# One weight load cut into two contraction halves, and two others joined, in a fused layernorm, state-space and SwiGLU kernel

## The chip, the cores and the metric

The kernel runs on one core of a Trainium2 chip. The metric is the device time of one execution in microseconds (us), taken as the median of several runs. A separate execution was recorded by the hardware profiler; all rows of the profile come from that one execution. Engines are named as the profile names them: PE (matrix products) with PEld (its weight loads), DVE (vector), ACT (activations and copies), POOL, and SP, which here only issues transfers. A "q" behind an engine's name (SPq) marks the issuing of a transfer and not the transfer itself.

## The reference

```python
x = A_x                                  # 1 x 2048 x 512, bf16
xn = _layernorm(x, axis=-1)
return x + _A_ref(xn, ...) + _B_ref(xn, w_gate, w_up, w_down)

def _B_ref(x, w_gate, w_up, w_down):     # 512 -> 1376 -> 512
    g = _silu(x @ w_gate)
    u = x @ w_up
    return (g * u) @ w_down
```

`_A_ref` is a diagonal complex state-space layer: an input projection with `B`, a recurrence over the 2048 positions, an output projection with `C`, and a skip term. Both branches read the same normalised input `xn`.

## The kernel before

The 2048 rows of x are cut into 16 tiles of 128 rows, and four tiles make a chunk of 512, so there are four chunks. The contraction over the 512 model columns is cut into four slices k = 0 to 3 of 128; `HK` is 2, half of them. The 1376 hidden columns make ten blocks `fi` of 128 and a last one of 96. The order on every engine is the order in which the program is written: nothing is moved later by a planner, and each engine works its list from top to bottom, waiting where an operand has not come.

**Loads.** Lines 123 to 142 issue the first loads. All but one go to SP: tile 0 of x (line 123), the gate weights of group 0 (`wg_g[0]`, blocks 0 and 1, line 126), the up weights of group 0 (`wu_g[0]`, line 127), tiles 2 and 3 of x (lines 128 and 129), then gate and up of group 1 (block 2, lines 130 and 131) and of group 2 (blocks 3 to 6, lines 136 and 137), and two transposing loads of `B_re` (line 139). Tile 1 of x goes out on ACT (line 125). The helper `load_w1` loads one group of one weight with one transfer; all its transfers carry line 113 in the profile. Each weight tile is laid out as partition, slice k, column. `load_mid` (line 144) follows later on SP, behind the transposing move of tile 3 (line 259). `load_late` (line 155) issues tiles 8 to 15 of x and then the down weights `wd_sb` in two transfers: blocks 0 to 4 and blocks 5 to 9 (lines 159 and 160). `wd_sb` is read by the output products (lines 566 and 592). Right behind `load_late` SP issues eight transposing loads of `C` (line 877).

**The head on PE.** While the first loads are under way PE runs dummy products (line 670). Tile 0 is normalised on DVE and transposed on PE (`xT_pe`, line 245), and its transpose is copied out by DVE (line 252) and ACT (line 254). Then the products of chunk 0 begin column by column through `head_mm` (line 693), whose arguments are the weight (0 gate, 1 up), the range of tiles, the slices k and the blocks:

```python
head_mm(0, 0, 1, range(0, HK), (0, 1))   # gate, k 0-1
head_mm(1, 0, 1, range(0, HK), (0,))     # up, k 0-1: first use of wu_g[0]
xT_pe(1)
rstd_act(2)
head_mm(0, 0, 1, range(HK, KD), (0, 1))
head_mm(1, 0, 1, range(0, HK), (1,))
head_mm(1, 0, 1, range(HK, KD), (0, 1))  # up, k 2-3
```

Behind them come the same products for tile 1, block 2 for tiles 0 and 1, the transposes of tile 2 (`xT_pe(2, on_dve=(0, 1))`, whose copies both go to DVE), the up products of block 2, and the products of tile 2. From line 763 on the blocks 3 to 6 follow at line 455, gate first, then up.

**The head on DVE.** In order: statistics of tiles 0 and 1, their normalisation (line 222), the statistics of tile 2 (line 205, with tile 2 of x as operand), half of the statistics of tile 3 (line 721), the normalisation of tile 2 (line 222), the other half for tile 3 (lines 723 and 724), and the two copies of the transposed tile 2 (line 252).

Of the kernel before, what the change touches and what calls it, by code (L numbers as in the profile page):

```python
# [23 lines left out]
def kernel(  # L24
# [17 lines left out]
    nc = tc.nc  # L42
# [9 lines left out]
    KD = D // 128  # L52
    HK = KD // 2
    NQ = Pst // 128
    FT = (F + 127) // 128
# [27 lines left out]
    wu_v = B_w_up.rearrange("(k p) f -> p k f", p=128)  # L83
# [5 lines left out]
    fgroups = [(0, 2), (2, 3), (3, 7), (7, FT - 1)]  # L89
    wg_g, wu_g = [], []  # L90
# [6 lines left out]
    wd_sb = const.tile([128, FT - 1, D], BF16, name="wd_sb")  # L97
# [13 lines left out]
    def load_w1(q, tiles, view, gi):  # L111
        a, b = fgroups[gi]
        q.dma_start(out=tiles[gi][:], in_=view[:, :, a * 128:min(F, b * 128)])  # L113
# [10 lines left out]
    nc.vector.memset(xall[:, 1, 0:D // 2], 0.0)  # L124
    nc.scalar.dma_start(out=xall[:, 1, :], in_=x_v[:, 1, :])
    load_w1(nc.sync, wg_g, wg_v, 0)
    load_w1(nc.sync, wu_g, wu_v, 0)
    nc.sync.dma_start(out=xall[:, 2, :], in_=x_v[:, 2, :])
    nc.sync.dma_start(out=xall[:, 3, :], in_=x_v[:, 3, :])
    load_w1(nc.sync, wg_g, wg_v, 1)  # L130
# [24 lines left out]
    def load_late():  # L155
        nc.scalar.dma_start(out=wu_last[:], in_=wu_v[:, :, FL:FL + LB])
        nc.sync.dma_start(out=xall[:, 2 * TPC:NT, :], in_=x_v[:, 2 * TPC:NT, :])
        wd_v = B_w_down[0:FL, :].rearrange("(k p) d -> p k d", p=128)
        for a, b in ((0, FT // 2), (FT // 2, FT - 1)):
            nc.sync.dma_start(out=wd_sb[:, a:b, :], in_=wd_v[:, a:b, :])  # L160


    ones = nc.const_aps.tensor(1.0, (128, CW), BF16)
# [692 lines left out]
    for part in range(2):  # L856
        for q in range(NQ):
# [10 lines left out]
           ["ln2"] * len(norm2) + ["ln3"] * (len(stats3) + len(norm3)))  # L868
    queue("cf", c_ops())
    load_late()  # L870
    for fi in range(G0, FT):
        gateup_tile(0, fi)
# [55 lines left out]
```

## Time and profile before

| | |
|---|---|
| median of 3 runs | 178.29 us (178.04 to 178.75) |
| the profiled execution | 178.63 us, of which the span from the first to the last instruction is 176.8 us |
| instructions | 2598 |
| busy: PE, PEld | 172.1 us, 83.4 us |
| busy: DVE, ACT, POOL | 153.8 us, 96.4 us, 51.8 us |
| granted TensorE clock | 1.000 |
| transfers | 16.36 MB in 31292 packets |

Rows of the timeline give start, duration, engine, line, operation, the tile written and the tile read, the shape and the number of merged instructions; what stands in brackets at the end is the idle time of the engine just before, and what ended it. Rows of transfers give the size and the time from issue to landing, that is, until the last of the data is in place. The chain of waits is followed back from the last instruction, at each step to what released it.

### The profile page before, as it was taken

To read this page: it belongs to the slowest core of one execution; us is meant where nothing else is said; L and a number is where in the kernel's file an instruction comes from. 1 tells how busy PE (TensorE), PEld (TensorE's weight loads), DVE (VectorE), ACT (ScalarE), POOL (GpSimd) and SP (SyncE) were. 2 spreads that over 40 slices of the span, in tenths; PEclk is the share of its full clock that TensorE was granted. 3 is DMA by queue.
4 is the path that set the end of the run, shared out by engine and by line. 5 is a ranking of instruction groups with operands and counts; after the bars stand their busy time and mean duration, and the time that the engine had idled before them with its cause. 6 is when DMAs were issued, how large, how long until landed. Compare 5 with 4: busy or idle time off the path is not lost.

```text
span 176.8 us, 2598 instructions
## 1 busy us (share of the span) xinstructions
PE 172.1 (97%) x939; PEld 83.4 (47%) x954; DVE 153.8 (87%) x235; ACT 96.4 (55%) x178; POOL 51.8 (29%) x86
## 2 busy tenths in 40 slices
PE   8999999999999999999999999999999999999993
PEld 3877544444444444444444444444444444444443
DVE  4779998999999997999999999999999999981033
ACT  5397899867698679714666661053866610001300
POOL 6050120001400220019998040058476510001410
PEclk9999999999999999999999999999999999999999
DMA  5998497995431013900000020029799300000652
GB/s 164 305 186 197 91 247 97 336 272 117 88 73 21 0 30 89 356 4 17 17 19 19 0 85 7 0 23 126 88 126 188 64 6 0 0 4 0 64 99 75
DMA packets 31292, 16.36 MB, mean 92 GB/s; under 512 B 20208, under 2 KB 31088, under 8 KB 31248
## 3 DMA queue, kind: packets, MB, share of 16 engines
q1 hardware_dynamic: 24704, 11.51, 27.5%
q0 software_dynamic: 5184, 4.07, 16.0%
q10 hardware_dynamic: 1392, 0.62, 1.2%
q8 instruction: 7, 0.11, 0.3%
q14 instruction: 5, 0.04, 0.1%
HBM read 8.33 MB, written 5.24 MB: 77 GB/s over the span
## 4 chain that ended last, share of the span: by engine, by line
PE 94%; DMA 2%; issue 1%; SPq 0%; DVE 0%
PE ps L455 35%; PE ps L604 16%; PE ps L380 16%; PE ps L566 10%; PE ps L592 10%; DMA wu<-in_B_w_up_dram 2%; PE ps L693 2%; PE ps L513 2%; PE ps L774 2%; PE ps L555 2%; PE ps L502 1%; PE ps L245 0%; SPq L113 0%; SPq L123 0%; DVE res L609 0%
## 5 line engine op out<-in xcount | busy, mean ns | idle before, releaser
L455 PE MATMUL ps<-xnT,wu 128*128 128x512 bf16 (+1 forms) x144 | 36.3, 373 | 0.2
L455 PE MATMUL ps<-xnT,wg 128*128 128x512 bf16 (+1 forms) x145 | 36.3, 373 | 0.2
L422 DVE TENSOR_TENSOR_SCAN g<-r_t,car,u 128x512 bf16<-128x512 f32 x24 | 28.8, 1263 | 0.0
L380 PE MATMUL ps<-xnT,BT 128*128 128x512 bf16 x126 | 28.2, 379 | 0.1
L604 PE MATMUL ps<-CF,wt 128*128 128x512 bf16 (+2 forms) x140 | 27.6, 355 | 0.4 <-issue 0.3
L474 ACT ACTIVATE guT<-ps 128x512 bf16<-128x512 f32 (+1 forms) x40 | 23.6, 590 | 5.9 <-PE ps L455 5.8
L475 ACT CAST u<-ps 128x512 bf16<-128x512 f32 (+1 forms) x40 | 23.0, 576 | 6.5 <-PE ps L455 6.4
L617 ACT CAST res<-ps 128x512 bf16<-128x512 f32 x12 | 6.7, 590 | 36.1 <-PE ps L604 26.8
L455 PEld LDWEIGHTS <-wu 128*128 128x128 bf16 x148 | 14.5, 98 | 16.6
L188 POOL DMA_DIRECT2D gu_rows<-ul x36 | 17.7, 499 | 15.8 <-DVE ul L490 15.8
L455 PEld LDWEIGHTS <-wg 128*128 128x128 bf16 x148 | 14.4, 98 | 16.5
L382 ACT CAST u<-ps 128x512 bf16<-128x512 f32 x32 | 18.2, 586 | 6.0 <-PE ps L380 5.9
L618 POOL DMA_DIRECT2D out_dram<-res x12 | 10.5, 1221 | 36.2 <-ACT res L617 36.1
L604 PEld LDWEIGHTS <-wt 128*128 128x128 bf16 x144 | 13.3, 98 | 15.0 <-issue 1.3
L380 PEld LDWEIGHTS <-BT 128*128 128x128 bf16 x128 | 12.5, 98 | 14.9 <-issue 0.3
L214 POOL TENSOR_TENSOR rstd<-ve,neg_half 128x2 f32<-128x2 f32 (+1 forms) x4 | 5.7, 1418 | 44.9 <-DVE ve L213 44.9
L592 PE MATMUL ps<-wd_sb,guT 128*128 128x512 bf16 x79 | 17.5, 379 | 0.1
L566 PE MATMUL ps<-wd_sb,guT 128*128 128x512 bf16 x79 | 17.4, 379 | 0.1
L470 DVE TENSOR_TENSOR guT<-guT,u 128x1024 bf16<-128x1024 bf16 x20 | 13.4, 678 | 0.0
L566 PEld LDWEIGHTS <-guT 128*128 128x128 bf16 x80 | 7.8, 98 | 9.5
L592 PEld LDWEIGHTS <-guT 128*128 128x128 bf16 x80 | 7.8, 98 | 9.5
L205 DVE BATCH_NORM_STATS2 stats<-xall 128x6 f32<-128x512 bf16 x14 | 9.5, 678 | 2.7 <-DMA xall<-in_A_x_dram 2.7
(125 smaller groups left out, 201.4 us busy)
## 6 DMA issues: line engine op xcount, KB each, us to landing
out_dram<-in_A_x_dram SPq DMA_DIRECT2D x1, 1536.0 KB, 6.9
out_dram<-res POOLq DMA_DIRECT2D x12, 128.0 KB, 3.5
out_dram<-xall POOLq DMA_DIRECT2D x3, 512.0 KB, 8.4
wd_sb<-in_B_w_down_dram SPq DMA_DIRECT2D x2, 640.0 KB, 8.2
xall<-in_A_x_dram SPq DMA_DIRECT2D x1, 1024.0 KB, 7.1
gu_rows<-ul POOLq DMA_DIRECT2D x36, 8.0 KB, 1.6
wg<-in_B_w_gate_dram SPq DMA_DIRECT2D x1, 512.0 KB, 4.7
wu<-in_B_w_up_dram SPq DMA_DIRECT2D x1, 512.0 KB, 5.5
```

Source lines behind the costliest of these rows:

```text
L188: nc.gpsimd.dma_start(out=gu_rows[c][i * RT:(i + 1) * RT, p, :], in_=product[p * RT:(p + 1) * RT, i * 128:(i + 1) * 128])
L380: nc.tensor.matmul(ps[:], lhsT=BT[:, part, k, q * 128:(q + 1) * 128], rhs=xnT[:, k, c * CW:(c + 1) * CW], start=(k == 0), stop=(k == KD - 1))
L382: nc.scalar.copy(out=u_tiles[c][:, part, q, :], in_=ps[:])
L422: V.tensor_tensor_scan(out=g()[:, part, q, :], data0=r_t[:, q:q + 1].to_broadcast([128, CW]), data1=u_tiles[c][:, part, q, :], initial=ini ...
L455: nc.tensor.matmul(ps[:fs, lo:hi], lhsT=wslice(groups, fi, k), rhs=xnT[:, k, c * CW + lo:c * CW + hi], start=(k == 0), stop=(k == KD - 1))
L470: products.append(lambda: V.tensor_tensor(out=g, in0=g, in1=u, op=ALU.mult))
L474: nc.scalar.activation(out=gu_tile(c)[:, fi, 0:hi], in_=psg[:, 0:hi], func=ACT.Silu)
L475: nc.scalar.copy(out=u_tile(c, fi)[:, fi % 2, 0:hi], in_=psu[:, 0:hi])
L566: nc.tensor.matmul(o[:], lhsT=gu_tiles[k][:, fi, i * 128:(i + 1) * 128], rhs=wd_sb[:, fi, :], start=(fi == 0), stop=False)
L592: nc.tensor.matmul(o[:], lhsT=gu_tiles[c][:, fi, i * 128:(i + 1) * 128], rhs=wd_sb[:, fi, lo:hi], start=(fi == 0), stop=False)
L604: nc.tensor.matmul(o, lhsT=w_tiles[c][:, part, q, i * 128:(i + 1) * 128], rhs=CF[:, part, q, lo:hi], start=(fresh and part == 0 and q == 0 ...
L618: nc.gpsimd.dma_start(out=out_v[:, n, :], in_=res[:], accum_op=ALU.add)
```

## The change

The load of the up weights of group 0 is cut along the contraction: slices k = 0 and 1 go with one transfer, slices 2 and 3 with a second one, both on SP, right behind one another, in the place of the single transfer. The down weights, ten blocks, come with one transfer in the place of two. Nothing else is changed.

```diff
     load_w1(nc.sync, wg_g, wg_v, 0)
-    load_w1(nc.sync, wu_g, wu_v, 0)
+    cut = fgroups[0][1] * 128
+    for ks in (slice(0, HK), slice(HK, KD)):
+        nc.sync.dma_start(out=wu_g[0][:, ks, :], in_=wu_v[:, ks, 0:cut])
     nc.sync.dma_start(out=xall[:, 2, :], in_=x_v[:, 2, :])
...
-        for a, b in ((0, FT // 2), (FT // 2, FT - 1)):
-            nc.sync.dma_start(out=wd_sb[:, a:b, :], in_=wd_v[:, a:b, :])
+        nc.sync.dma_start(out=wd_sb[:], in_=wd_v)
```

## The prediction

> **What bounds the kernel now.** I read the page first, then the chain of waits, then the timeline of the first 13 us engine by engine, because the larger edit acts there.
>
> ```profile
> PE 172.1 (97%) x939; PEld 83.4 (47%) x954; DVE 153.8 (87%) x235; ACT 96.4 (55%) x178; POOL 51.8 (29%) x86
> ```
>
> ```profile
> 1.66 4.36 DMA wu<-in_B_w_up_dram
> 6.02 0.05 issue
> 6.07 0.28 PE ps L693 x2
> ...
> 10.52 5.20 PE ps L455 x32
> ```
>
> PE is busy nearly all the time. The chain of waits (start, duration, what) says the same: once the first up weights have landed at 1.66 + 4.36 = 6.02, it runs over PE. So the end moves with PE's list, and a microsecond saved or lost by PE in the head is kept, as long as nothing else runs late in between. The only transfer that the chain names is the one that the change cuts in two. PE's weight loads show what it costs:
>
> ```profile
> 5.18 0.40 PEld L693 LDWEIGHTS <-wg 128*128 128x128 bf16 x4
> 6.06 0.11 PEld L693 LDWEIGHTS <-wu 128*128 128x128 bf16 x2 [0.48 <-DMA wu<-in_B_w_up_dram]
> 6.13 0.27 PEld L245 LDWEIGHTS <-xall 128*128 128x128 bf16 x4
> ...
> 8.19 0.32 PEld L245 LDWEIGHTS <-xall 128*128 128x128 bf16 x4
> ...
> 10.30 0.64 PEld L455 LDWEIGHTS <-wg 128*128 128x128 bf16 x5
> ```
>
> The gate weights are through at 5.18 + 0.40 = 5.58; then PEld stands still for 0.48 us until the up weights are there. That is the whole of what the first edit can win. Two later rows matter: at 8.19 the transposes of tile 2 begin, and at 10.30 the first gate weights of group 2 are taken.
>
> **Part 1, the early half.** SP's issues and the landing times (KB and median us from issue to landing):
>
> ```profile
> 0.74 0.40 SPq L123 DMA_DIRECT2D xall<-in_A_x_dram  x1
> 1.20 0.42 SPq L113 DMA_DIRECT2D wg<-in_B_w_gate_dram  x1
> 1.66 0.51 SPq L113 DMA_DIRECT2D wu<-in_B_w_up_dram  x1
> 2.21 0.50 SPq L128 DMA_DIRECT2D xall<-in_A_x_dram  x1
> ...
> 4.26 0.51 SPq L113 DMA_DIRECT2D wg<-in_B_w_gate_dram  x1
> 5.16 0.37 SPq L113 DMA_DIRECT2D wu<-in_B_w_up_dram  x1
> 5.57 3.21 SPq L139 DMA_TRANSPOSE BT<-in_A_B_re_dram  x2
> 9.53 1.23 SPq L259 DMA_TRANSPOSE xnT<-xall  x1
> ```
>
> ```profile
> wg<-in_B_w_gate_dram SPq DMA_DIRECT2D x1, 512.0 KB, 4.7
> wu<-in_B_w_up_dram SPq DMA_DIRECT2D x1, 512.0 KB, 5.5
> ...
> wg<-in_B_w_gate_dram SPq DMA_DIRECT2D x1, 256.0 KB, 3.9
> ```
>
> Gate group 0 lands at 1.20 + 3.9 = 5.10 and up group 0 at 6.02, so the 256 KB of the second took 0.92 us behind the first. Half of them should be there at 5.10 + 0.46 = 5.56; with the 0.04 us that PE took from landing to weight load, PEld can go on at 5.60 in place of 6.06. PE comes forward by **0.46 us** at this point. The second half still lands at about 6.02. PE needs it after twelve more weight loads (two up, four transposes, four gate, two up); at 0.27 us for four, as in the row at 6.13, these take about 0.8 us from 5.60 on, so the second half is in time.
>
> **What is late next.** The advance meets the chain of tile 2 on DVE:
>
> ```profile
> 5.09 0.41 DVE L222 TENSOR_SCALAR xall<-xall,mv,rstd 128x512 bf16<-128x512 bf16 x1
> 6.46 0.69 DVE L205 BATCH_NORM_STATS2 stats<-xall 128x6 f32<-128x512 bf16 x1 [0.96 <-DMA xall<-in_A_x_dram]
> ...
> 7.64 0.41 DVE L222 TENSOR_SCALAR xall<-xall,mv,rstd 128x512 bf16<-128x512 bf16 x1
> ...
> 8.61 0.49 DVE L252 COPY xnT<-ps 128x256 bf16<-128x256 bf16 x2
> ```
>
> Tile 1 is normalised at 5.50, before PE would ask for it at about 5.67, so the transposes of tile 1 follow the advance. Tile 2 does not: DVE waits 0.96 us for its data, begins at 6.46, and ends its normalisation at 7.64 + 0.41 = 8.05. PE took it at 8.19. With an advance of 0.46 us it would ask at 7.73 and wait until 8.05 plus some 0.06 us of signalling (an estimate: tile 1's first use in the same manner), that is 8.11. Of 0.46 us there remain 0.08. The next meeting is closer still:
>
> ```profile
> 9.02 0.50 PE L693 MATMUL ps<-xnT,wg 128*128 128x128 bf16 x6
> ```
>
> These products read the first copy of the transposed tile 2. DVE makes it at 8.61, behind its own statistics of tile 3, which do not move; half of the pair, about 0.29 us with its tail, brings it to 8.90, and PE can begin at 8.96 in place of 9.02. **The first edit is thus worth 0.06 us**, if tile 2 lands when it did.
>
> Does it? Between the old transfer and tile 2 stands one more transfer with the same bytes. The 256 KB of up group 0 took 0.92 us, and tile 2's 128 KB were in use 0.44 us later (6.02 to 6.46). Twice 0.44 is 0.88, so a transfer in a filled queue shows no charge of its own beside its bytes. Bounds for the extra delay: below, zero, since the bytes ahead of tile 2 are the same; above, 0.44 us, as if the added transfer cost a whole 128 KB. I take zero, as the two steps agree; at 0.44 the first edit would lose 0.44 - 0.08 = 0.36 us.
>
> The page "DMA: Bandwidth & Descriptors" of the Trainium skill, in its section on rules for kernel authors, speaks against the cut: many small transfers should be merged, and full bandwidth wants 1 MiB or more in each; its anatomy of one DMA gives a fixed cost of about 2.0 us to each. Were that paid in line, tile 2 would come 2.0 us later and the kernel take about 180.2; the 0.44 us step beside the 0.92 us step says that here it overlaps.
>
> **Part 2, one more issue on SP.** An issue takes 0.42 to 0.51 us plus a gap of about 0.05, so everything behind it on SP goes out about 0.55 us later. Tile 2 was issued 4.25 us before its use (2.21 to 6.46), behind a filled queue, so this hides there, and I take it to hide for tile 3 and group 1 behind it as well. Group 2 is different. In the row at 5.16 SP had waited:
>
> ```profile
> SPq L113 <- DMA wg<-in_B_w_gate_dram: 0.4, 1, 0.4
> ```
>
> With ACT's one load it is the tenth load of the program and the landing that it waits for is that of the second; I read that as a limit of eight under way, an inference. With one more load ahead, the tenth is the gate load of group 2, which moves from 4.26 to about 5.16 instead of to 4.81; the up load follows at about 5.7. Costs: gate group 2 landed at 4.26 + 4.7 = 8.96, 1.34 us before its use at 10.30. If it moves with its issue it lands at 9.86: hidden. If it takes as long as the up load did, 5.16 + 5.5 = 10.66: 0.42 us late for a need at 10.24. Lower end zero, upper 0.42; I take zero, as the queue still holds group 1 while group 2 is issued. Up group 2 lands at 10.66 at present and is used here:
>
> ```profile
> 12.80 2.54 PEld L455 LDWEIGHTS <-wu 128*128 128x128 bf16 x16
> ```
>
> That leaves 2.1 us of cover for a delay of 0.55 to 0.9. The two transposing loads of B move by about 0.6 us; SP ended them at 8.78 and then stood until 9.53 for DVE's tile 3, 0.75 us, so from line 259 on SP is where it was.
>
> **Part 3, the down weights.**
>
> ```profile
> L592 PE MATMUL ps<-wd_sb,guT x30: 379/379/380, 63.6 to 69.8; 128*128 128x512 bf16 x30
> L160 SPq DMA_DIRECT2D wd_sb<-in_B_w_down_dram x2: 523/549/575, 29.5 to 30.2; - x2
> ...
> DMA to landing us min/median/max: 7.6/8.2/8.7
> ```
>
> The second transfer lands at 30.2 + 8.7 = 38.9 and the first reader runs at 63.6: a cover of 24.7 us. One issue of about 0.55 us goes away on SP, where it sets nothing. Whether joined or not, the 1280 KB are ahead of the loads of C, so those gain at most the 0.55 us and lose nothing. Worth zero; without that cover the first reader would lose the 1.1 us (7.6 against 8.7) by which the first half can be used earlier.
>
> **The sum.** Against the profiled execution, 176.8 us of span and 1.83 us around it: 176.8 - 0.06 + 0 + 0 = 176.74, plus 1.83 makes 178.57. The profiled run stands 0.34 us above the median of the three runs, 178.29; by the same shift the median is 178.23, said as **178.2 us**.
>
> **The rivals.**
>
> *The whole wait is won.* If tile 2 comes 0.4 us earlier in most executions than in the profiled one, nothing catches the advance and 0.46 us are won: 177.8. For it: landing times in the head are those of one execution. Against it: tile 2 lies behind the same bytes as the up weights, so what brings one forward brings the other.
>
> *The cut does nothing.* If the products wait for the tile as a whole, the first up product still waits for 6.02, and the time is 178.3. Against it:
>
> ```profile
> 2.87 0.69 DVE L205 BATCH_NORM_STATS2 stats<-xall 128x6 f32<-128x512 bf16 x1 [1.75 <-DMA xall<-in_A_x_dram]
> ```
>
> DVE reads tile 0 of `xall` at 2.87, over 3 us before tile 2 of the same buffer is in use; parts of a buffer are waited for one by one.
>
> *Group 2 comes late (the slower side).* SP holds the gate load of group 2 until gate group 0 has landed. It decides once that load lands after 10.24. At the landing time of its neighbour PE waits 0.42 us at line 455, nothing behind gives it back, and the time is 178.29 + 0.36 = 178.65. For it: the wait is in the trace, and only its place has to move. Against it: 1.34 us of slack, of which the known delay takes 0.9.
>
> *Every transfer pays its start in line.* Tile 0 had nothing ahead and was in use 2.87 - 0.74 = 2.13 us after its issue; less 0.44 us for its bytes, 1.7 us are start. If the added transfer pays that in line, tile 2 lands 1.7 us later, DVE's chain and PE with it, and 1.6 us are lost: 179.9. It decides from a delay of about 0.1 us of tile 2. Against it stand the two steps of part 1. [...]
>
> **How the numbers follow.** Forecast 0.60; whole wait won 0.09; no effect 0.10; group 2 late 0.15; start paid in line 0.04; the rest, 0.02, is a loss or gain that I do not see. A measurement of this kernel tells about 0.5%, 0.9 us, from no change. The first four cases all lie within that, which makes 0.94 with little lost to their tails; the fifth is slower; I give same 0.91, slower 0.06 and faster 0.03. The range reaches from the whole wait won, 177.8, to group 2 late with 0.15 us of tile 2's delay on top, 178.8. The three runs before cover 178.04 to 178.75, so the range is hardly wider than their own scatter.
>
> **What would show it.** Right: two rows for the up weights at about 1.66 and 2.2 on SP; the first up weight loaded near 5.6; a new idle time of PEld of about 0.4 us before the transposes of tile 2, ended by DVE, and these at about 8.1; line 455 from about 10.24; the issue of gate group 2 at about 5.16. Wrong: tile 2's statistics later than 6.55 (the added transfer has a price), a wait for `wg` at line 455 (group 2), the transposes of tile 2 near 7.75 (the whole wait won), the first up weight still at 6.06 (no effect), or any wait for `wd_sb` at line 592.

## The result and the profile after

| | before | after |
|---|---|---|
| median, 22 runs of each side by side | 178.31 us (177.97 to 178.85) | 178.72 us (178.37 to 179.51) |
| ratio of after to before | | 1.0025 (95% interval 1.0015 to 1.0035) |
| the profiled execution | 178.63 us, span 176.8 | 178.37 us, span 176.6 |

The changed kernel is slower by 0.25%, 0.41 us. That is less than the 0.5% that the prediction took as the least difference a measurement tells, but the interval, which stays above 1, leaves no doubt of the sign. The two profiled executions stand the other way round: before's lies 0.32 us above its median, and after's is the lowest of its 22 runs. So the spans can't be subtracted. What can be read are the waits.

The chain of waits after (start, duration, what), from its transfer on; ahead of it stand only SP's issues:

```profile
4.18 4.11 DMA wu<-in_B_w_up_dram
8.34 1.95 PE ps L694 x28
10.29 5.20 PE ps L456 x32
```

The transfer is still a load of up weights, but another one. Before, it was the load of group 0, issued at 1.66; now it is the load of group 1, issued at 4.18 and landed at 4.18 + 4.11 = 8.29. PE's weight loads after, in the timeline (lines are one higher than before):

```profile
5.07 0.38 PEld L694 LDWEIGHTS <-wg 128*128 128x128 bf16 x4
5.41 0.15 PEld L694 LDWEIGHTS <-wu 128*128 128x128 bf16 x2
5.62 0.23 PEld L246 LDWEIGHTS <-xall 128*128 128x128 bf16 x4
...
7.64 0.32 PEld L246 LDWEIGHTS <-xall 128*128 128x128 bf16 x4
7.92 0.10 PEld L276 LDWEIGHTS <-prm_rows 128*128 128x128 bf16 x1
8.34 0.33 PEld L694 LDWEIGHTS <-wu 128*128 128x128 bf16 x4 [0.32 <-DMA wu<-in_B_w_up_dram]
...
10.07 0.64 PEld L456 LDWEIGHTS <-wg 128*128 128x128 bf16 x5
```

The cut did what it says. The first up weights are taken at 5.41 in place of 6.06, with no idle time ahead of them, and the transposes of tile 2 begin at 7.64 in place of 8.19. Then PEld stands for 0.32 us for the up weights of group 1, and line 456 begins at 10.07, against 10.30 at line 455 before. SP's issues after:

```profile
1.66 1.02 SPq L129 DMA_DIRECT2D wu<-in_B_w_up_dram  x2
2.72 0.47 SPq L130 DMA_DIRECT2D xall<-in_A_x_dram  x1
3.23 0.43 SPq L131 DMA_DIRECT2D xall<-in_A_x_dram  x1
3.71 0.43 SPq L113 DMA_DIRECT2D wg<-in_B_w_gate_dram  x1
4.18 0.51 SPq L113 DMA_DIRECT2D wu<-in_B_w_up_dram  x1
4.74 0.52 SPq L113 DMA_DIRECT2D wg<-in_B_w_gate_dram  x1
```

Every issue behind the cut goes out about half a microsecond later: tile 2 at 2.72 (2.21 before), up group 1 at 4.18, gate group 2 at 4.74 (4.26).

### The profile page after: what moved, and what is told of

Its sections match the earlier page's. It is cut to its first block, busy times and chain, and to the rows that moved or that the text cites. A ratio compares the mean times of both kernels' runs of the same rounds, so it can differ in the third digit from the quotient of the medians.

```text
span 176.6 us, 2613 instructions
## 1 busy us (share of the span) xinstructions
PE 172.6 (98%) x954; PEld 83.0 (47%) x954; DVE 153.8 (87%) x235; ACT 96.6 (55%) x178; POOL 51.9 (29%) x86
## 4 chain that ended last, share of the span: by engine, by line
PE 94%; DMA 2%; SPq 2%; issue 0%; DVE 0%
PE ps L456 35%; PE ps L605 16%; PE ps L381 16%; PE ps L593 10%; PE ps L567 10%; DMA wu<-in_B_w_up_dram 2%; PE ps L514 2%; PE ps L775 2%; PE ps L556 2%; PE ps L694 1%; PE ps L503 1%; SPq L129 1%; SPq L113 0%; SPq L130 0%; SPq L131 0%
## 5 line engine op out<-in xcount | busy, mean ns | idle before, releaser
L605 PE MATMUL ps<-CF,wt 128*128 128x512 bf16 (+2 forms) x144 | 28.2, 356 | 0.0
```

The costliest lines, as they stand in the source:

```text
L605: nc.tensor.matmul(o, lhsT=w_tiles[c][:, part, q, i * 128:(i + 1) * 128], rhs=CF[:, part, q, lo:hi], start=(fresh and part == 0 and q == 0 ...
```

## The experiments

Two theories came out of the traces. *Theory A*: the added issue on SP makes group 1's up load late for PE; the cut itself costs nothing. *Theory T*, formed after the first four runs: the number of transfers in the program decides how long the program takes to end behind its last product. Their rivals: the cut itself is what delays the loads behind it, joining the down weights costs or wins time somewhere, or the spread of runs is all there is. The expectations on record say for which of them they speak.

One finding makes the runs comparable. From the first product of block 3 (line 455 in before, 454 to 458 in the others) to the end of the last product it is 163.73 us to within 0.02 in the profiles of both kernels and of e1 to e8, e10 and e12 (164.31 in e9, 164.89 in e11). So a span is the start of block 3, plus 163.73, plus what follows the last product. This table has these parts for every profile. "Up group 1" gives the issue of that load and the landings of the first, the twelfth and the last of its 16 parts, from the landing events of the trace; "gate group 2" gives the landing of that load's last part; "tail" is the span behind the last product; the ratio is to runs of before taken beside each kernel.

| kernel | issue added on SP ahead of group 1 | up group 1: issue; first, 12th, last part | gate group 2 | block 3 | tail | ratio (interval) |
|---|---|---|---|---|---|---|
| before | | 3.71; 6.62, 7.15, 7.50 | 8.99 | 10.36 | 2.75 | 1 |
| after | 1 | 4.18; 6.75, 7.62, 8.29 | 9.79 | 10.13 | 2.75 | 1.0025 (1.0015 to 1.0035) |
| e1 | 1 | 4.19; 6.80, 7.75, 8.50 | 10.04 | 10.33 | 3.42 | 1.0058 (1.0042 to 1.0074) |
| e2 | | 3.70; 6.74, 7.12, 7.22 | 9.41 | 10.04 | 2.82 | 1.0014 (1.0001 to 1.0026) |
| e3 (after again) | 1 | 4.18; 6.50, 7.50, 8.27 | 10.55 | 10.59 | 2.74 | 1.0020 (1.0009 to 1.0032) |
| e4 (before again) | | 3.71; 6.80, 7.04, 7.42 | 9.59 | 10.23 | 2.75 | 1.0003 (0.9985 to 1.0020) |
| e5 | 1 | 4.19; 6.78, 7.17, 8.49 | 10.03 | 10.32 | 2.74 | 1.0021 (1.0008 to 1.0034) |
| e6 | | 3.67; 6.74, 7.02, 7.66 | 9.48 | 9.85 | 2.75 | 0.9993 (0.9980 to 1.0005) |
| e7 | | 3.71; 6.75, 7.12, 7.43 | 9.74 | 9.79 | 3.42 | 1.0045 (1.0029 to 1.0060) |
| e8 | | 3.71; 6.70, 7.08, 7.29 | 9.55 | 10.43 | 2.75 | 1.0019 (1.0007 to 1.0032) |
| e9 | 2 | 4.88; 7.01, 7.34, 8.76 | 10.49 | 10.59 | 3.20 | 1.0052 (1.0035 to 1.0069) |
| e10 | one fewer | 3.16; 6.80, 7.29, 8.03 | 9.55 | 11.50 | 2.75 | 1.0069 (1.0044 to 1.0095) |
| e11 | 1 | 4.19; 6.71, 7.80, 8.20 | 10.21 | 10.26 | 2.75 | 1.0077 (1.0059 to 1.0094) |
| e12 (e6 again) | | 3.67; 6.73, 7.07, 7.49 | 10.30 | 10.35 | 2.75 | 1.0003 (0.9989 to 1.0018) |

### The change in its two halves, and both kernels again

e1 makes the cut alone and leaves the down weights in two transfers; e2 joins the down weights alone; e3 and e4 are after and before, profiled once more.

```diff
 # e1: in load order, on before
-    load_w1(nc.sync, wu_g, wu_v, 0)
+    cut = fgroups[0][1] * 128
+    for ks in (slice(0, HK), slice(HK, KD)):
+        nc.sync.dma_start(out=wu_g[0][:, ks, :], in_=wu_v[:, ks, 0:cut])
 # e2: in load_late, on before
-        for a, b in ((0, FT // 2), (FT // 2, FT - 1)):
-            nc.sync.dma_start(out=wd_sb[:, a:b, :], in_=wd_v[:, a:b, :])
+        nc.sync.dma_start(out=wd_sb[:], in_=wd_v)
```

> Only the cut of the first up load is done; the down weights keep their two transfers. Theory A (one more issue ahead makes the up load of group 1 land late, and PE waits for it at the up products of block 2): the whole loss is here, +0.3 to +0.5 us against before, and the profile shows PEld waiting 0.2 to 0.6 us for wu at the helper head_mm ahead of the second 128x256 group, with the up load of group 1 landing after 7.9 us. Rival B (the joined down weights cost the time): within 0.1 us of before.

> Only the down weights are joined; the first up load stays one transfer. Theory A: within 0.15 us of before, no wait for wd_sb. Rival B: +0.3 to +0.5 us, with a later landing of the loads behind it or a slower output part.

> The changed kernel as it is, for a second profile and more times. Theory A: +0.3 to +0.5 us against before, a PEld wait for wu of 0.2 to 0.6 us at the up products of block 2 again. If the wait in the first profile was an accident of one execution, it is absent here and the time is still about +0.4.

> The kernel before as it is, for a second profile. Theory A: no wait for wu at block 2; the up load of group 0 lands near 5.5 us and not 6.02 (the 6.02 of the first profile was one late execution), so PE waits for it at most 0.15 us; time within 0.1 us of before. Rival C (the profile of before was typical): the first up load lands near 6.0 again and PE waits 0.4 to 0.5 us for it.

Beside a before of 178.13, the medians were 179.20 (e1), 178.41 (e2), 178.62 (e3) and 178.20 (e4). The result repeats: e3 is slower by 0.49. The cut alone costs 1.07, more than twice what the pair costs and far beyond the +0.3 to +0.5 expected of it, so the joined down weights give something back that a cover of 24.7 us had made look worthless. Joined alone they win nothing: e2 lies 0.28 above before, where at most 0.15 was expected, with an interval barely above 1.

The up load of group 1 lands late in e1 and e3 as in after. What PE then waits for differs. The timeline of e3, whose PE was late by itself, shows no wait for those weights, but one at the next group:

```profile
10.59 2.39 PEld L456 LDWEIGHTS <-wg 128*128 128x128 bf16 x16 [0.16 <-DMA wg<-in_B_w_gate_dram]
```

That is the load of gate group 2, landed at 10.55. In e1 the wait for up group 1 was 0.14 us, short of the 0.2 to 0.6 expected. In e4 the first up weights, landed at 5.84, were waited for only half as long as in the first profile of the same kernel, though longer than the 0.15 that Theory A allowed (timeline):

```profile
5.88 0.13 PEld L693 LDWEIGHTS <-wu 128*128 128x128 bf16 x2 [0.23 <-DMA wu<-in_B_w_up_dram]
```

and e2's timeline, with the same head, has no such wait:

```profile
5.63 0.23 PEld L692 LDWEIGHTS <-wu 128*128 128x128 bf16 x2
```

### The issue without the cut

e5 leaves the first up load whole and puts a transfer of 2 KB behind it on SP, into a tile that nobody reads. The down weights are joined as in after.

```diff
     load_w1(nc.sync, wu_g, wu_v, 0)
+    pad = const.tile([128, 8], BF16, name="pad")
+    nc.sync.dma_start(out=pad[:], in_=x_v[:, 2, 0:8])
```

> The first up load stays whole; behind it SP issues a tiny transfer (16 bytes for each partition into a tile that nobody reads), and the down weights are joined, so that the number of transfers is that of before. Theory A (the added issue on SP makes the up load of group 1 late): group 1 up lands at 8.0 to 8.5 us instead of 7.2 to 7.5, PE waits for it, the products of block 3 start at 10.1 to 10.4, and the time is +0.3 to +0.5 us. Rival D (the cut itself, two halves in place of one, makes it late): group 1 up lands within 0.2 us of before, no wait at block 2, time within 0.15 us of before.

178.65 against 178.16 for before: +0.49, as much as after and e3. No weight load is cut, and up group 1 again lands at 8.49. PE's timeline:

```profile
8.53 0.33 PEld L694 LDWEIGHTS <-wu 128*128 128x128 bf16 x4
```

PE takes these weights 0.04 us after they land. What costs is the issue, for which 2 KB do as well as the 128 KB of a half.

### The cut without the issue

e6, repeated as e12, is after with the second half of the first up load issued by ACT, behind its one load of tile 1.

```diff
-    for ks in (slice(0, HK), slice(HK, KD)):
-        nc.sync.dma_start(out=wu_g[0][:, ks, :], in_=wu_v[:, ks, 0:cut])
+    for q, ks in ((nc.sync, slice(0, HK)), (nc.scalar, slice(HK, KD))):
+        q.dma_start(out=wu_g[0][:, ks, :], in_=wu_v[:, ks, 0:cut])
```

> The changed kernel, but the second half of the first up load is issued by ACT, so SP issues as many loads ahead of group 1 as before. Theory A: group 1 up lands at 7.2 to 7.6 us, no wait for it, the products of block 3 start at 9.7 to 9.9, and the time is 0.3 to 0.6 us below the changed kernel, at or a little below before. Rival D: as slow as the changed kernel, +0.3 to +0.5 us.

> The second half of the first up load issued by ACT, once more, to see whether it beats the kernel before. Theory A: group 1 up lands by 7.7 us again, no wait for it, the products of block 3 start at 9.7 to 9.9; time 0 to 0.15 us below before. If the first time was luck, the median is 0.2 us or more above before.

178.14 against 178.16 (e6) and 178.39 against 178.31 (e12): both the same as before. Up group 1 landed at 7.66 (e6; 7.2 to 7.6 was expected) and 7.49 (e12). Block 3 began at 9.85 in e6, as expected, but at 10.35 in e12, where gate group 2 landed only at 10.30. e6 is the cleanest pair to after, since both begin the transposes of tile 1 at 5.62 and go on at the same pace. Its weight loads in the timeline:

```profile
7.68 0.32 PEld L246 LDWEIGHTS <-xall 128*128 128x128 bf16 x4
7.96 0.10 PEld L276 LDWEIGHTS <-prm_rows 128*128 128x128 bf16 x1
8.02 0.37 PEld L694 LDWEIGHTS <-wu 128*128 128x128 bf16 x4
...
9.79 0.97 PEld L456 LDWEIGHTS <-wg 128*128 128x128 bf16 x7
```

At 7.96 it is 0.04 behind after (7.92); the next row stands at 8.02, without a wait, where after has 8.34; and block 3 follows at 9.79 in place of 10.07. That is the price of the late load with all else alike: 0.28 us. With e5, this shows from both sides that the added issue costs the time, and not the cut. It also shows that the cut wins nothing over before even where it is free.

### Why the issue could not hide

The prediction took the queue behind the cut to be filled, so that a later issue would only shorten a wait in the queue. The view of windows gives for a stretch: its bounds and length, the busy time of PE, PEld, DVE, ACT and POOL, the granted clock, the share of the 16 engines that were moving data (over 1 where packets overlap), and GB/s. Without the added issue, first before (e4), then e6:

```profile
4.00:8.00 4.00, 4.00 (x49) 3.25 (x48) 3.06 (x11) 2.00 (x8) 0.30 (x1) 1.00 1.08 287
4.00:8.00 4.00, 4.00 (x54) 3.58 (x53) 3.32 (x12) 1.87 (x7) 0.31 (x1) 1.00 1.06 291
```

and with it, first after, then e5:

```profile
4.00:8.00 4.00, 3.71 (x55) 3.21 (x53) 3.61 (x12) 2.06 (x8) 0.31 (x1) 1.00 0.96 244
4.00:8.00 4.00, 4.00 (x49) 3.57 (x48) 2.99 (x11) 1.91 (x7) 0.31 (x1) 1.00 0.99 242
```

In these four microseconds the share is 1.03 to 1.10 in the six profiles without an added issue that keep before's other loads in place (before, e2, e4, e6, e7, e12), and 0.93 to 0.99 in the five with one (after, e1, e3, e5, e11); the rate is 272 to 302 GB/s and 225 to 245. So the engines moved less, but they were near full in both. The rates alone would say too much, because the packets differ: in before's trace between 4 and 8 us those of 256 bytes (group 1) took 18 ns in the median and those of 1,024 bytes (x, group 2) 46 ns, so a stretch full of group 1 has a low rate with busy engines. An issue in this part of SP's list takes 0.42 to 0.52 us, the one for 2 KB in e5 and the one for 256 KB in before 0.51 each, and by the prediction's own steps the bytes of 128 KB take 0.44 to 0.46 us. SP therefore has nothing in hand, and one more issue leaves the engines with less to do. This fits the shares; no run tests it by itself. The Trainium skill, page "DMA: Bandwidth & Descriptors", section "Issuing engines are not separate DMA queues", holds the time to initiate a transfer to be usually small beside the transfer; for the 128 KB loads of this head the two are alike.

How 0.47 us of issue become 0.8 to 1.0 us of landing isn't settled. The first part of the load landed as early as before (6.75 against 6.62 to 6.80), the twelfth 0.35 to 0.7 us later where the weights are cut (but not in e5), and the last one later still in all of them. One suspect was the pair of transposing loads of B right behind; e11 is after with that pair moved behind the transposing move of tile 3.

> The changed kernel with the first two transposing loads of B moved behind the transposing move of tile 3, so SP is free after the loads of group 2. If those transposing issues hold back the tail of the up load of group 1, it lands before 7.9 us and PE does not wait for it. If the added issue alone sets it, it lands at 8.1 to 8.5 as before. The total time is no measure here, since the later loads of B come late.

Up group 1 still landed at 8.20, so the transposes aren't it. PE took it without an idle wait, and the wait came, as in e3, at gate group 2 (timeline):

```profile
10.26 0.44 PEld L455 LDWEIGHTS <-wg 128*128 128x128 bf16 x4 [0.19 <-DMA wg<-in_B_w_gate_dram]
```

Its total, 179.59 (two runs), says nothing here: from the start of block 3 (10.26) to the last product it needs 164.89 us, 1.16 more than the others.

### Two issues, and other places for an issue

e9 is before with two of the 2 KB transfers, the down weights in two as in before.

```diff
+    for i in range(2):
+        pad = const.tile([128, 8], BF16, name=f"pad{i}")
+        nc.sync.dma_start(out=pad[:], in_=x_v[:, 2, 0:8])
```

> Two tiny transfers behind the whole first up load, and the down weights in two transfers as before: two issues more on SP, two transfers more in all. Theory A: group 1 up lands later than with one added issue (8.7 us or more), the products of block 3 start at 10.5 to 11.0 instead of 9.8 to 10.3. Theory T: the last store uses the second counter that SP waits for at the end, so the span behind the last product is 3.3 to 3.4 us. Together +1.3 to +1.8 us. Rival: delays do not add, block 3 starts by 10.4.

179.10 against 178.17, +0.93, and so less than was expected. Up group 1 landed at 8.76 and gate group 2 at 10.49, each later than with one added issue, but the second issue added far less than the first. (Up group 1 also went out later than its place in SP's list, at 4.88, when gate group 0 had landed at 4.86.) Block 3 began at 10.59, and 0.58 us more were lost in that execution behind it.

e8 is after with tile 3 of x issued by ACT, so that the loads of group 1 go out when they did before.

```diff
-    nc.sync.dma_start(out=xall[:, 3, :], in_=x_v[:, 3, :])
+    nc.scalar.dma_start(out=xall[:, 3, :], in_=x_v[:, 3, :])
```

> The changed kernel with the load of tile 3 of x issued by ACT instead of SP, so that both halves stay on SP and group 1 is issued as early as before. Theory A: group 1 up lands at 7.2 to 7.6 us, no wait for it, time 0.3 to 0.6 us below the changed kernel. Rival D: no better than the changed kernel.

Up group 1 landed at 7.29, in time, as Theory A has it; its forecast of the time failed: 178.66 against 178.16. Tile 2, still behind the added issue and now behind tile 3 as well, landed at 6.69. PE's timeline:

```profile
8.36 0.23 PEld L246 LDWEIGHTS <-xall 128*128 128x128 bf16 x4 [0.68 <-DVE xall L223]
```

That is the meeting with DVE's chain of tile 2 that the prediction had described. The head has three limits close together, tile 2, the up weights of group 1 and the gate weights of group 2 (e3, e11), and one issue more makes one or another of them late.

e10 is before with the whole first up load on ACT.

```diff
-    load_w1(nc.sync, wu_g, wu_v, 0)
+    load_w1(nc.scalar, wu_g, wu_v, 0)
```

> The kernel before with the whole first up load issued by ACT instead of SP: one issue fewer ahead of tile 2 and group 1, the number of transfers as before. Theory A: tile 2 and group 1 land up to 0.5 us earlier, no wait for them; the products of block 3 start at 9.7 to 9.9; time 0 to 0.2 us below before. Rival: the up load, now mixed with SP's loads of x on the same engines, lands later than 5.5 us and PE waits for it: +0.1 to +0.4 us.

179.46 against 178.17, +1.29: the gain that Theory A forecast did not come, and the loss is far beyond the rival's +0.1 to +0.4. The timeline of PE's weight loads:

```profile
7.21 0.11 PEld L693 LDWEIGHTS <-wu 128*128 128x128 bf16 x2 [1.66 <-DMA wu<-in_B_w_up_dram]
```

The load, issued at about the same time as before, landed at 7.17 in place of 5.3 to 6.0. Tiles 2 and 3, issued behind it by SP, landed ahead of it, at 6.42 and 6.88: nothing keeps SP's later loads behind it.

### The end of the program

e1 and after have the same head, and e1's tail is 0.67 us longer. e7 changes the number of transfers far from the head: before, with the down weights in three.

```diff
-        for a, b in ((0, FT // 2), (FT // 2, FT - 1)):
+        for a, b in ((0, 4), (4, 7), (7, FT - 1)):
```

> The kernel before with the down weights in three transfers, so one transfer more in all and nothing changed in the head. Theory T (the time behind the last product depends on the number of transfers modulo eight, since SP at the end waits for eight counters in a fixed order and one more transfer puts the last store on the first of them): span behind the last product 3.4 us instead of 2.75, time +0.6 to +0.7 us, head as before. Rival: the +1.0 of the cut alone came from its head; then this one is within 0.15 us of before.

178.97 against 178.16, +0.81, with the earliest block 3 of all profiles (9.79) and a tail of 3.42. Where it comes from stands in the view of SP's waits (in total, times, longest), at the end of the program. After:

```profile
SPq L924 <- PEq L924: 0.7, 2, 0.5
...
SPq L924 <- DMA out_dram<-res: 0.5, 2, 0.4
```

e7:

```profile
SPq L923 <- DMA out_dram<-res: 1.0, 1, 1.0
...
SPq L923 <- PEq L923: 0.4, 2, 0.2
```

e1:

```profile
SPq L925 <- DMA out_dram<-res: 1.0, 1, 1.0
...
SPq L925 <- PEq L925: 0.4, 2, 0.2
```

The last store of the result is waited for once, for 1.0 us, in place of 0.5 in two pieces. SP's instructions there show why: it ends by waiting for the counters of the transfers, in a fixed order. The time at which SP passed each wait, with the counter's number, from the records of the trace:

```
e4  last store issued 174.31 on counter 118
    174.71 (110)  174.78 (101)  174.84 (102)  174.91 (111)  174.97 (112)  175.03 (113)  175.17 (115)  175.58 (116)  175.79 (118)
e1  last store issued 174.42 on counter 101
    174.81 (110)  175.90 (101)  175.96 (102)  176.03 (111)  176.09 (112)  176.15 (113)  176.21 (115)  176.27 (116)  176.36 (117)
```

The counters are handed out in turn to the transfers of SP and ACT, so their number decides which one the last store gets. On a late one (118) the walk over the others, about 0.065 us each, is done while the store is still on its way. On an early one (101) SP stands until the store has landed and walks over the others afterwards. From the issue of the store to the last of these waits it takes 175.79 - 174.31 = 1.48 us in e4 and 176.36 - 174.42 = 1.94 in e1; that is 0.46 of the 0.67. The other 0.2 lie between the last wait and the end (0.92 us in e4, 1.12 in e1), and why isn't shown. One transfer more than before gives 3.42 (e1, e7), the same number 2.74 to 2.75 (the other profiles), one fewer 2.82 (e2, last store on 116), two more 3.20 (e9, on 102; 3.3 to 3.4 was expected). So Theory T holds, and the pair of edits is bound together by it: the cut adds a transfer and joining takes one away. Of the 1.07 us of e1, 0.67 lie here and 0.40 are left for the head, which is the 0.41 of the pair. Two differences stay without a cause: e2 lost 0.28 with only 0.07 in its tail (its interval begins at 1.0001), and e7 lost 0.81, 0.14 beyond its tail.

## Why the prediction was wrong, point by point

The forecast was 178.2 us, 0.06 us won; it was 178.72, 0.41 us lost. The range of 177.8 to 178.8 held it, and so did the chance for less than 0.5%; the sign was wrong. That the range held it is in part luck: its upper end was priced from group 2 and tile 2, and the loss in after came from group 1, for which the prediction had no price.

*The step that failed* is in part 2: one more issue "hides there, and I take it to hide for tile 3 and group 1 behind it as well". For tile 2 and tile 3 it held. For group 1 the delay was put at nothing without a reason of its own: for up group 1 the prediction didn't set the landing against the need. Before's timeline has the need:

```profile
8.53 0.37 PEld L693 LDWEIGHTS <-wu 128*128 128x128 bf16 x4
```

The load landed at 7.50, so its cover was 1.03 us. The landing moved by 0.8 to 1.0, which alone would nearly have fitted. But this need was a late one, since PE had waited 0.48 us for the first up weights; where they come in time, the same products stand at 7.96 (e7), 8.02 (e6) or 8.21 (e2), and the load, landing at 8.20 to 8.50 with the added issue, is too late or just in time. e5 shows the loss with the issue alone, e6 and e12 show it gone with the issue elsewhere. The premise, "behind a filled queue", did not hold: with the added issue the engines had less to do, a share of 0.93 to 0.99 in place of 1.03 to 1.10.

*The size of that loss* can be put together only as an estimate. In each of the five profiles with one added issue a late landing is the last thing that PE waits for ahead of block 3: up group 1 in after, e1 and e5 (0.32, 0.14 and 0.14 us), gate group 2 in e3 and e11 (0.16 and 0.19). Block 3 then begins at 10.33 on average. In the six profiles without one it begins at 10.10, only 0.22 us earlier, where the medians differ by 0.41 to 0.49. But before's two profiles are slower than before's medians. By the sum above, with some 1.78 us between a span and its time, medians of 178.16 and 178.31 stand for a block 3 at about 9.90 and 10.05, and against these the loss is 0.28 to 0.43. The heads of single executions scatter by 0.5 us, so a remainder of some 0.1 stays open.

*Part 1* was right in its mechanism: parts of the buffer are waited for one by one, the first half was in use at 5.41 (5.60 forecast), the second in time, and tile 2 wasn't delayed (its statistics at 5.87, against 6.46 before). The rival that every transfer pays its start in line is out: the halves were issued 0.55 us apart and landed 0.77 apart, at 4.83 and 5.60, not 1.7 or 2.0. (The section that the prediction names for the 2.0 us is about transfers issued by gpsimd, POOL here; these are SP's.) One small slip of the part: a delay of 0.44 us would lose 0.38 by its own later figure of 0.06 us, not 0.36. But the 0.48 us of waiting on which the part rested was that of one execution: 0.23 in e4 and none in e2 and e7. There was little to win, and the prediction's own remark, that landing times in the head are those of one execution, should have been used on the wait as well.

*What is late next* was right too, but not second in line: tile 2's chain shows as a limit in e8, and in e9 by 0.22 us. In after PE didn't wait for it, since tile 2 was early (DVE's timeline):

```profile
5.87 0.69 DVE L206 BATCH_NORM_STATS2 stats<-xall 128x6 f32<-128x512 bf16 x1 [0.30 <-DMA xall<-in_A_x_dram]
...
7.05 0.41 DVE L223 TENSOR_SCALAR xall<-xall,mv,rstd 128x512 bf16<-128x512 bf16 x1
...
8.06 0.49 DVE L253 COPY xnT<-ps 128x256 bf16<-128x256 bf16 x2
```

*Group 2* was the rival nearest to the measured time, 178.65, by the right cause, SP's list moved back, but by a load that was only at times the one that came late. The gate of group 2 landed at 9.79 in after, hidden, and was waited for in e3 (0.16 us) and e11 (0.19). So the zero taken for it was too low as well. The issue at 5.16 didn't come: SP sent it at 4.74, as gate group 0 had landed by 4.38 in that execution and there was nothing to wait for. In e8, where that landing was at 4.98, the issue stood until 5.00, so the inference of a wait for an earlier landing holds; the trace shows the later load on the counter that the earlier one had.

*Part 3* has a wrong zero. The cover of the down weights was there and no product waited for them. But the transfer that was taken away is worth 0.67 us at the end of the program, beside the cut that adds one. The prediction looked for users of the data, and the effect doesn't depend on the data at all.

*The median before* was taken from a profile shifted by 0.34 us; with the 22 runs the shift is 0.32, so this step was sound.

## What to carry to other kernels

In this head, fed by transfers of some 128 KB that SP issues back to back, an added issue of 2 KB made a load behind it land as late as one of 128 KB did. Where loads are issued like that, set the landing of every load behind an added issue against the moment it is needed, not only that of the next one. A wait in the first microseconds should be seen in several profiles before an edit is built on it. And when two versions differ in their number of transfers, look at the tail behind the last product before the difference is put down to the edit.

## What the runs showed of the hardware

**The number of transfers moves the end of the program**: 2.75 to 3.42 us behind the last product, by which counter the last store falls on. No row of the costliest groups shows it; only SP's waits do.

**PE's pace in the head doubles at a different moment in each execution.** A step of four products takes about 0.42 us, start to start, before that point and 0.22 us after it. The trace's record of the granted clock begins, with 1.0, at the same moment: at 3.86 us in after, 5.29 in e7, 6.05 in before and 6.73 in e3. The timeline of e3:

```profile
5.73 0.47 PEld L246 LDWEIGHTS <-xall 128*128 128x128 bf16 x4
6.16 0.47 PEld L694 LDWEIGHTS <-wg 128*128 128x128 bf16 x4
...
7.00 0.27 PEld L694 LDWEIGHTS <-wg 128*128 128x128 bf16 x4
```

In after, four loads from 5.62 on are done in 0.23 us already. The view of windows shows 1.00 ahead of the moment too, but no record stands behind it there. The Trainium skill, page "TensorE: Matmul & The Clock Gate", section "What's actually happening", says that the window which decides on the full clock runs freely, so that the number of slow products differs from run to run; that agrees with these moments, and no run here shows the window itself. In the profiles without an added issue that do not wait for the first up weights, block 3 follows the moment: 9.79 (e7, 5.29), 9.85 (e6, 5.52), 10.04 (e2, 5.78), 10.35 (e12, 6.21, of which 0.07 is a wait for gate group 2).

**Two issuing engines keep no order between their loads.** The same 256 KB, asked for at the same time, landed at 5.3 to 6.0 from SP's list and at 7.17 from ACT's (e10), while half of it on ACT landed in time (5.25 in e6).
